# Seven products instead of eight in part of an MLP's first layer, at the end of a fused attention and MLP kernel

## The chip, the cores and the metric

The kernel runs on one core of one Trainium2 chip. A core has engines that work at the same time and wait for one another by semaphores: TensorE (PE in the profile) multiplies matrices into PSUM, a small memory of eight banks, each with room for 128 x 512 f32; VectorE (DVE) and ScalarE (ACT) compute elementwise and read PSUM; GpSimd (POOL) works on SBUF and issues loads; SyncE (SP) issues stores. Each engine takes its instructions strictly in the order in which they were written. The metric is the device time of one execution in microseconds; lower is better. The kernel before takes 332.02 us, the median of six runs from 331.83 to 332.23.

## The reference

```
k_all = concat(beacon_k, k);  v_all = concat(beacon_v, v)       # 16 beacons, then 576 keys
scores = q @ k_all.T / 8, causal for the 576 keys               # 8 batches, 8 heads, 576 x 592, D = 64
x = softmax(scores) @ v_all                                     # to 4608 tokens x 512
h = x @ w_in                                                    # 512 x 2048: the first layer
g = h * sigmoid(1.702 * h)
out = g @ w_out                                                 # 2048 x 512: the second layer, f32
```

## The kernel before, in words

The attention is cut into 16 sets: a batch and four of its eight heads each. A set's scores are computed in chunks of up to 512 columns into one score tile `s` of four banks (`e_qk`, line 458), ScalarE takes the exp of a chunk into the set's buffer `E` in f16 (`e_exp`, line 469; three buffers `E` in all), GpSimd sets the part above the diagonal to zero (line 490), VectorE adds up rows (`e_zadd`, line 508), and TensorE multiplies by ones, for the row sums, and by the values (`e_av`, line 545). VectorE inverts the sums and writes the scaled result to `xT` (`e_norm`, line 580), which is the transposed input of the MLP in f16. There are 55 chunks.

The MLP works on ten groups of tokens: groups 0 and 1 of 256, groups 2 to 9 of 512. In the first layer (`e_m1`, line 604) a group has sixteen n-tiles of 128 columns of `w_in`, each a sum over four k-tiles: four matmuls of 128 x 128 weights by 512 tokens, into one PSUM bank. ScalarE applies the gelu out of the bank into `g` (`e_gelu`, line 625). Group 8 needs tokens of the last batch, group 9 all of it, so both start after nearly all of the attention.

The second layer of groups 2 to 9 already uses Strassen's scheme in Winograd's form: `g` (512 tokens x 2048) and `w_out` (2048 x 512) are cut into two by two quarters, and seven products of quarters stand in for eight. VectorE makes four sums of quarters of `g` in pieces (`e_s`, line 669) and, once, four sums of the weights (`e_t`). A product (`e_prod`, line 718) is sixteen matmuls of 256 columns into one bank. The first product is copied by ScalarE (`e_half`, line 729), and seven VectorE joins (`e_join`, line 734) add the products up to the four quarters of the output, which SyncE stores.

The PSUM banks: four for the score tile, four (`RING`) in a ring that the attention's values, first-layer tiles and second-layer products share.

What runs when is fixed ahead by a planner in the same file (`Plan`). Every operation is entered with its engine, an estimated duration, the operations it depends on, a priority and a due time; `run` then simulates the engines, picks for each the next operation, and the program is emitted in that order. What matters here:

- `quota`: the matmuls of a group's first layer (kind `m1`) are let in once a number of score chunks (`QUOTAS`, for groups 2 to 9) has been issued and the group's input is there; then the planner is `inside`, issues all sixteen n-tiles in a row and no scores. A group is also let in when TensorE would stand idle for more than `IDLE` ns.
- `choose` picks TensorE's next operation: scores first, then values that have been ready for long, then, outside of a group, `m1` and second-layer operations (`m2`, four matmuls each) by turns.
- At most two second-layer banks are open at a time (`allowed`).
- A ring bank becomes free once the operations that close its tile are planned (`ring_free`).
- VectorE takes its operations by priority; it stays idle for up to `NEAR` ns when an urgent one is about to be ready.
- Loads of q, k, v and the transposes have due times that follow a line from `T_ATT0` to `T_ATT1` over the chunks (`due_of`).

Of the kernel before, what the change touches and what calls it, by code (L numbers as in the profile page):

```python
# [12 lines left out]

NEAR = 500
IDLE = 800

# [8 lines left out]
class Plan:  # L25
# [5 lines left out]
    def __init__(self, ring):  # L31
        self.ops = []
        self.bank = [None] * ring
        self.tiles = {}
        self.closers = {}
        self.quota = {}
# [17 lines left out]

    def ring_free(self):
        best = None
        for i, key in enumerate(self.bank):
            t = 0
            for c in self.closers[key] if key is not None else ():
                t = None if t is None or c.start is None else max(t, c.end + 60)  # L60
            if t is not None and (best is None or t < best[0]):
                best = (t, i)
        return best

    def run(self):
# [7 lines left out]
        table, due_of_table = "e", {"e": 0, "g": 0}  # L73
        group, inside, ntile, nchunk = min(self.quota), False, 0, 0
        firsts = {}
        for o in self.ops:
            if o.kind == "m1":
                firsts.setdefault(o.pr, o)

        left_of = {}  # L80
# [4 lines left out]
        def allowed(o):  # L85
            if o.kind == "m2" and o.ring not in self.tiles:
                if sum(left_of[k] > 0 for k in self.tiles if k in left_of) >= 2:
                    return False
            if o.kind == "m1":
                return o.pr < group or (o.pr == group and (inside or group not in self.quota))  # L90
            if o.kind == "qk":
                return not inside
            if o.table is not None and o.table != table:
                return due_of_table[table] == 0
            return True
# [3 lines left out]
        while todo:  # L99
            best = None  # L100
            if not inside and group in self.quota:
                f = firsts[group]
                inside = nchunk >= self.quota[group] and f.left == 0
            slot = self.ring_free()
            ringt = slot[0] if slot else None
            for e, cand in avail.items():
                t = None
                for o in cand:
                    if not allowed(o):
                        continue  # L110
                    r = max(o.ready, o.due)
                    if o.ring is not None and o.ring not in self.tiles:
                        if ringt is None:
                            continue
                        r = max(r, ringt)
                    if t is None or r < t:
                        t = r
                if t is not None:
                    t = max(t, free[e])
                    if best is None or t < best[0]:  # L120
                        best = (t, e)
# [8 lines left out]
            for o in avail[e]:  # L130
                if not allowed(o):
                    continue
                r = max(o.ready, o.due)
                if o.ring is not None and o.ring not in self.tiles:
                    if ringt is None:
                        continue
                    r = max(r, ringt)
                if r <= t:
                    ok.append(o)
            if e == "PE":  # L140
                o = self.choose(ok, t, mode, last, free, inside)
            else:
# [7 lines left out]
            if e == "PE":  # L150
                if o.mode != mode:
                    dur += 95 + 0.75 * tail / 2.4
                mode, last, tail = o.mode, o.kind, o.tail
                if o.ring is not None and o.ring not in self.tiles:
                    self.tiles[o.ring] = slot[1]
                    self.bank[slot[1]] = o.ring
            if o.kind == "m1":
                ntile += 1 if o.pr == group else 0
                if inside and ntile == 16:
                    group, inside, ntile = group + 1, False, 0  # L160
            if o.kind == "m2":
# [29 lines left out]
    def choose(self, ok, t, mode, last, free, inside):  # L191
# [13 lines left out]
        if qk:  # L205
            return qk
        late = first(("av",), lambda o: o.ready + 7000 <= t)
        if late:
# [10 lines left out]
def kernel(  # L219
# [41 lines left out]
    sp = ctx.enter_context(tc.tile_pool(name="sp", bufs=3))  # L261
    pss = ctx.enter_context(tc.tile_pool(name="pss", bufs=1, space=bass.MemoryType.PSUM))
    psu = ctx.enter_context(tc.tile_pool(name="psu", bufs=1, space=bass.MemoryType.PSUM))

    keep = cst.tile([P, P], F16, tag="keep", name="keep")
# [4 lines left out]
    NPL, NPE, GEL = 2, 10, 2  # L270
    QUOTAS = (19, 28, 38, 42, 48, 55, 55, 55)
    HM, HN = 256, NNT // 2
    xT = cst.tile([P, NKT, XR], F16, tag="xT", name="xT")
    sA = [cst.tile([P, HN, HM], F16, tag=f"sA{i}", name=f"sA{i}") for i in range(3)]
# [82 lines left out]

    plan = Plan(RING)

    def ring_tile(key):  # L360
        if key not in rings:
            i = plan.tiles[key]
            rings[key] = psu.tile([P, 512], F32, tag=f"u{i}", name=f"u{i}")
        return rings[key]
# [51 lines left out]
    def f32(ap):  # L416
        return ap.bitcast(F32)
# [173 lines left out]
    NG = len(GROUPS)  # L591

    def e_m1(g, n0, n1):
        t0, t1 = GROUPS[g]
        w = t1 - t0
        if g not in gts:
            gts[g] = gp.tile([P, NNT, 512], F16, tag="g", name="g")
        u = ring_tile(("m1", g, n0))
# [77 lines left out]
    def e_t(i, eng):  # L676
# [9 lines left out]
        else:  # L686
            add(eng, t3, b22, b12, ALU.subtract)

    def quarter(g, i, j):
        return gts[g][:, HN * j : HN * (j + 1), HM * i : HM * (i + 1)]  # L690
# [54 lines left out]

    T_ATT0, T_ATT1 = 17000, 249000
    NCH0 = 4 * HS
# [113 lines left out]
    def values(s):  # L861
# [7 lines left out]
        for i in range(1, NJ if whole else 0):  # L869
            w = S - s0s[i]  # L870
            deps = after(s, wcol[i], wcol[i] + w) + (after(s, Z0, S) if i == 1 else [])
            sums.append(
                op("DVE", 75 + 0.517 * 4 * w, deps + sums[-1:], lambda i=i: e_zadd(s, i), pr=3, name="zadd")
            )
# [72 lines left out]
    m1s, done = {}, {}  # L947
    SQ, SDVE, TDUE = 2, 0, 60000

# [8 lines left out]
    def products(g):  # L958
        eng = "POOL" if g < SDVE else "DVE"
        sd = {}  # L960
        for n0 in range(0, HN, SQ):
            n1 = n0 + SQ
            prev = []
            for i in range(4):
                deps = prev + done.get(g - 1, [])
                for n in range(n0, n1):
                    deps += [gates[(g, n)], gates[(g, n + HN)]]
                d = 336
# [7 lines left out]
        def prod(p):  # L976
            prev = []
            for n0 in range(0, HN, SQ):
# [3 lines left out]
                else:  # L982
                    deps += [gates[(g, n + (HN if p in (2, 4) else 0))] for n in range(n0, n0 + SQ)]
                if rhs[p] is not None:
# [37 lines left out]
        ends[g] = c12  # L1022

    def mlp(g):
        if g == NPL and NPL < NPE:
# [15 lines left out]
        for n0 in firsts:  # L1041
            n1 = n0 + n
            key = ("m1", g, n0)
            pe = op(
# [55 lines left out]
    for o in done.get(NPL - 1, []) + done.get(NPL - 2, []) if tds else ():  # L1100
        also(tds[3], o)
    plan.quota.update(zip(range(GEL, NG), QUOTAS))
    order = plan.run()
# [31 lines left out]
```

## Time and profile before

| | |
|---|---|
| median of the runs | 332.02 us |
| the profiled execution | 331.98 us, its span 330.3 us |
| TensorE busy | 311.5 us, 94% |
| VectorE busy | 237.7 us, 72% |
| ScalarE busy | 203.6 us, 62% |
| GpSimd busy | 116.7 us, 35% |
| first matmul | at 8.6 us |
| first layer of group 8 | 268.1 to 282.0 us |
| first layer of group 9 | 288.2 to 302.0 us |
| last product ends | 326.4 us |

A group of instructions in the profile is named by its line in the code, its engine and operation, then what it writes and reads by the program's names with shapes, then how many there were. TensorE's granted clock is full throughout. Matmuls are pipelined, so one that starts every 109 ns is listed with a longer duration of its own.

### The profile page before, as it was taken

The page shows a single profiled execution, that of the slowest core. Times are in us where ns is not written, and L with a number is a line of the kernel's source. Part 1 is how long each engine was busy: PE and PEld are TensorE (multiplying, and loading weights), DVE is VectorE, ACT ScalarE, POOL GpSimd, SP SyncE. Part 2 cuts the span into 40 slices and gives each one's busy share as a digit, 9 for nine tenths or more (in the row PEclk, how much of TensorE's full clock was granted, in tenths as well). Part 3 has the DMA queues.
Part 4 walks back from the last instruction along what each step waited for, and adds up shares of the span by engine and source line. Part 5 has one row for each costly group of instructions (what it writes and reads, how often), then busy time and mean ns, then how long its engine had stood idle before and what let it go on. Part 6 is the DMA issues. An engine that isn't in the chain of part 4 may idle for free. (4 is left out here: it accounts for less than half of the span.)

```text
span 330.3 us, 9837 instructions
## 1 busy us (share of the span) xinstructions
PE 311.5 (94%) x4288; PEld 211.0 (64%) x4288; DVE 237.7 (72%) x478; ACT 203.6 (62%) x234; POOL 116.7 (35%) x178
## 2 busy tenths in 40 slices
PE   0699899999999999999999999999999999999995
PEld 0477566545885467746878887447774664746884
DVE  3847958796998787987999589978896630460484
ACT  1576487787767786787758586858677426175000
POOL 8764557573238205360427046702422000000000
PEclk9999999999999999999999999999999999999999
DMA  7999999569017903392149623930020000110122
GB/s 127 161 206 208 200 175 151 87 108 131 20 48 134 150 2 82 89 134 44 40 102 126 87 51 89 130 81 2 34 97 2 2 32 2 44 52 2 65 96 95
DMA packets 58219, 28.81 MB, mean 87 GB/s; under 512 B 41280, under 2 KB 53568, under 8 KB 58176
## 3 DMA queue, kind: packets, MB, share of 16 engines
q0 software_dynamic: 47552, 18.49, 47.8%
q1 hardware_dynamic: 10560, 9.69, 8.9%
q8 instruction: 33, 0.54, 0.6%
q14 instruction: 10, 0.08, 0.1%
q10 hardware_dynamic: 64, 0.01, 0.0%
HBM read 37.22 MB, written 9.44 MB: 141 GB/s over the span
## 5 line engine op out<-in xcount | busy, mean ns | idle before, releaser
L604 PE MATMUL u<-xT,w 128*128 128x512 f16 (+1 forms) x704 | 130.8, 343 | 2.1 <-DVE g L637 1.1
L469 ACT ACTIVATE E<-s 128x2048 f16<-128x2048 f32 (+4 forms) x66 | 98.8, 1514 | 42.9 <-PE s L458 42.2
L604 PEld LDWEIGHTS <-w 128*128 128x128 f16 x704 | 67.9, 98 | 58.5 <-issue 3.3
L625 ACT ACTIVATE g<-u 128x512 f16<-128x512 f32 x128 | 74.4, 599 | 43.2 <-PE u L604 43.1
L490 POOL TENSOR_SCALAR_AFFINE_SELECT E<-E 128x512 f16<-128x512 f16 (+3 forms) x78 | 52.0, 688 | 121.9 <-ACT E L469 118.2
L734 DVE SCALAR_TENSOR_TENSOR osb<-u,osb 128x512 f32<-128x512 f32 x56 | 37.4, 680 | 40.5 <-PE u L718 26.9
L718 PEld LDWEIGHTS <-g 128*128 128x128 f16 x512 | 48.7, 98 | 7.3 <-issue 0.2
L458 PE MATMUL s<-qT,kT 32*128 32x32 f16 (+20 forms) x1376 | 36.0, 235 | 12.0 <-DVE qT L429 8.6
L718 PE MATMUL u<-w,g 128*128 128x256 f16 x384 | 46.0, 273 | 0.0
L458 PEld LDWEIGHTS <-kT 32*128 32x128 f16 x1376 | 26.2, 96 | 29.2 <-issue 15.1
L718 PEld LDWEIGHTS <-sA 128*128 128x128 f16 x384 | 36.4, 98 | 4.9
L718 PE MATMUL u<-tB,sA 128*128 128x256 f16 x256 | 31.3, 273 | 0.0
L389 POOL DMA_DIRECT2D vb<-in_v_dram x32 | 27.3, 871 | 2.8 <-DMA kn<-in_k_dram 1.7
L545 PE MATMUL u<-E,vb 128*32 128x352 f16 (+8 forms) x928 | 27.7, 267 | 0.0
L580 DVE TENSOR_TENSOR xT<-u,rz 128x352 f16<-128x352 f32 (+2 forms) x52 | 24.9, 519 | 1.7 <-PE u L545 1.1
L508 DVE TENSOR_TENSOR zs<-zs,E 128x1344 f16<-128x1344 f16 (+2 forms) x36 | 23.2, 645 | 2.7 <-DVE zs L508 0.5
L429 DVE STREAM_TRANSPOSE kT<-kn 128x576 f32<-128x576 f32 x16 | 20.1, 1258 | 4.9 <-PE s L458 2.8
L545 PEld LDWEIGHTS <-vb 128*32 128x32 f16 (+1 forms) x928 | 20.2, 98 | 5.4 <-issue 1.3
L429 DVE STREAM_TRANSPOSE qT<-qn 128x576 f32<-128x576 f32 x16 | 20.0, 1248 | 2.7 <-PE s L458 1.8
L669 DVE TENSOR_TENSOR sA<-g 128x512 f16<-128x512 f16 x32 | 12.8, 417 | 12.3 <-ACT g L625 12.0
L557 DVE STREAM_TRANSPOSE zt<-u 128x352 f32<-128x352 f32 (+2 forms) x32 | 13.8, 459 | 9.0 <-PE u L545 8.9
L718 PE MATMUL u<-tB,g 128*128 128x256 f16 x128 | 16.3, 273 | 0.0
(44 smaller groups left out, 229.6 us busy)
## 6 DMA issues: line engine op xcount, KB each, us to landing
out_dram<-osb SPq DMA_DIRECT2D x36, 256.0 KB, 2.2
kn<-in_k_dram POOLq DMA_DIRECT2D x16, 288.0 KB, 6.0
qn<-in_q_dram POOLq DMA_DIRECT2D x16, 288.0 KB, 6.6
vb<-in_v_dram POOLq DMA_DIRECT2D x24, 128.0 KB, 5.5
w<-in_moe_w_in_dram POOLq DMA_DIRECT2D x8, 256.0 KB, 8.9
w<-in_moe_w_out_dram POOLq DMA_DIRECT2D x4, 512.0 KB, 14.2
vb<-in_v_dram POOLq DMA_DIRECT2D x8, 112.0 KB, 3.6
vb<-in_v_dram POOLq DMA_DIRECT2D x8, 80.0 KB, 5.4
```

The costliest lines, as they stand in the source:

```text
L389: nc.gpsimd.dma_start(out=t[0 : hi - lo, j, h0:h1, :], in_=v[b, h0:h1, lo:hi, :].rearrange("h n d -> n h d"),)
L429: nc.vector.transpose(out=f32(dst.rearrange("p n e -> p (n e)")).rearrange("p (r t) -> p t r", t=TR), in_=f32(src[:, :]).rearrange("p (t c ...
L458: nc.tensor.matmul(sc[:, h, o : o + w], kT[s % NB2][r : r + 32, j * P : (j + 1) * P, d], qT[s % NB2][r : r + 32, a : a + w, d], start=(d = ...
L469: nc.scalar.activation(out=Es[s][:, :, c0:c1], in_=ss[i][:, :, o : o + c1 - c0], func=AFT.Exp, scale=0.125,)
L490: nc.gpsimd.affine_select(out=blk, in_=blk, compare_op=ALU.is_ge, fill=0.0, base=off + (Nb if j == 0 else 0), pattern=[[0, Q], [1, w]], ch ...
L508: nc.vector.tensor_tensor(out=t, in0=E[:, :, Z0:S] if i == 1 else t, in1=E[:, :, wcol[i] : wcol[i] + S - a], op=ALU.add,)
L545: nc.tensor.matmul(u[32 * h : 32 * h + 32, a:e], lhs, src[0:kw, h, col : col + e - a], start=first, stop=last,)
L580: nc.vector.tensor_tensor(out=xT[:, 2 * hs + x : 2 * hs + x + n, t0 : t0 + w], in0=rings[("av", s, x, half)][:, 0 : n * w].rearrange("p (n ...
L604: nc.tensor.matmul(u[:, o + a - t0 : o + e - t0], w1t[:, kp, nt * P : (nt + 1) * P], xT[:, kp, a % XR : (e - 1) % XR + 1], start=(kp == 0) ...
L625: nc.scalar.activation(out=gts[g][:, n0:n1, 0:w], in_=rings[("m1", g, n0)][:, 0 : n * w].rearrange("p (n w) -> p n w", n=n), func=AFT.Gelu ...
L718: nc.tensor.matmul(u[:, HM * mt : HM * (mt + 1)], lhs[:, n, mt * P : (mt + 1) * P], rhs[:, n, :], start=(n == 0 and mt == 0), stop=(n == H ...
L734: nc.vector.scalar_tensor_tensor(out=osbs[(g, dst)][:, :], in0=rings[("p", g, p)][:, :], scalar=scale_of(g), in1=osbs[(g, src)][:, :], op0 ...
```

## The change

Blocks of the first layer of groups 8 and 9 are computed by the same scheme of seven products. A block `d` is the n-tiles 2d, 2d+1, 2d+8 and 2d+9 for the group's 512 tokens. Its quarters are: two k-tiles of `w_in` by two n-tiles, and two k-tiles of `xT` by 256 tokens. `FIRST` lists the blocks: 0 and 2 of group 8, 0, 1 and 2 of group 9; the other three blocks of these groups stay as they were.

- Four sums of halves of `w_in` (128 x 2048, f16) are made once, and four sums of quarters of `xT` (128 x 512, f16) per group, on VectorE. They lie in the `E` buffers of the last sets, once these are no longer read.
- A product (`e_first`) is four matmuls of 256 columns into one bank.
- ScalarE copies the first product to SBUF in f32 (`e_fcopy`). Seven VectorE joins (`e_fjoin`) per block add the others to it, in f32 in the last `E` buffer. Four gelus per block (`e_fgelu`) read the joined quarters from SBUF instead of from a bank.
- The products have four banks of their own, keys that begin with `n`: the score tile's pool is closed and a pool of four one-bank tiles is opened in its place, free for the planner 200 ns after the last exp (`gate`).
- From group 8 on (`MIX`), first-layer operations are allowed whenever they are ready, and `choose` no longer puts them ahead of the second layer.
- Other constants: `NEAR`, `IDLE`, `QUOTAS`, `T_ATT0` and `T_ATT1`, the time after which waiting values go first, `TDUE` (due time of the sums of `w_out`), and the estimate for the row sums.

```diff
-NEAR = 500
-IDLE = 800
+NEAR = 560
+IDLE = 3000
+MIX = 8
+LATE1 = 0
...
-    def ring_free(self):
+    def ring_free(self, late):
         best = None
-        for i, key in enumerate(self.bank):
-            t = 0
+        if late and self.gate.start is None:
+            return None
+        for i in range(self.ring, self.ring + 4) if late else range(self.ring):
+            key = self.bank[i]
+            t = self.gate.end + 200 if late else 0
...
             if o.kind == "m1":
+                if group >= MIX:
+                    return True
                 return o.pr < group or (o.pr == group and (inside or group not in self.quota))
...
-                o = self.choose(ok, t, mode, last, free, inside)
+                o = self.choose(ok, t, mode, last, free, inside and (group < MIX or LATE1))
...
-        late = first(("av",), lambda o: o.ready + 7000 <= t)
+        late = first(("av",), lambda o: o.ready + 5000 <= t)
...
-    QUOTAS = (19, 28, 38, 42, 48, 55, 55, 55)
+    QUOTAS = (20, 27, 33, 33, 47, 54, 55, 55)
     HM, HN = 256, NNT // 2
+    FIRST = {8: (0, 2, ), 9: (0, 1, 2, )}
...
             i = plan.tiles[key]
-            rings[key] = psu.tile([P, 512], F32, tag=f"u{i}", name=f"u{i}")
+            if i >= RING and not late_s:
+                scores.close()
+                late_s.append(ctx.enter_context(tc.tile_pool(name="psl", bufs=1, space=bass.MemoryType.PSUM)))
+            rings[key] = (psu if i < RING else late_s[0]).tile([P, 512], F32, tag=f"u{i}", name=f"u{i}")
...
+    def wq(i, j):
+        return w1t[:, 2 * j : 2 * j + 2, DFF // 2 * i : DFF // 2 * (i + 1)]
+
+    def xq(g, i, j):
+        t0 = (GROUPS[g][0] + HM * j) % XR
+        return xT[:, 2 * i : 2 * i + 2, t0 : t0 + HM]
...
+    def e_first(g, d, p):
+        u = ring_tile(("n", g, d, p))
+        lhs, rhs = {
+            1: (wq(0, 0), xq(g, 0, 0)),
+            2: (wq(0, 1), xq(g, 1, 0)),
+            3: (wsum(2), xq(g, 1, 1)),
+            4: (wq(1, 1), xsum(g, 2)),
+            5: (wsum(0), xsum(g, 0)),
+            6: (wsum(1), xsum(g, 1)),
+            7: (wsum(3), xsum(g, 3)),
+        }[p]
+        for t in range(2):
+            n = (2 * d + t) * P
+            for k in range(2):
+                nc.tensor.matmul(u[:, HM * t : HM * (t + 1)], lhs[:, k, n : n + P], rhs[:, k, :], ...)
+
+    def e_fcopy(g, d):
+        nc.scalar.copy(out=part(d, "m"), in_=rings[("n", g, d, 1)][:, :])
+
+    def e_fjoin(g, d, p, src, dst):
+        nc.vector.tensor_tensor(
+            out=part(d, dst), in0=rings[("n", g, d, p)][:, :], in1=part(d, src), op=ALU.add
+        )
...
-    T_ATT0, T_ATT1 = 17000, 249000
+    T_ATT0, T_ATT1 = -1000, 245000
...
-                op("DVE", 75 + 0.517 * 4 * w, deps + sums[-1:], lambda i=i: e_zadd(s, i), pr=3, name="zadd")
+                op("DVE", 75 + 0.6 * 4 * w, deps + sums[-1:], lambda i=i: e_zadd(s, i), pr=3, name="zadd")
...
-    SQ, SDVE, TDUE = 2, 0, 60000
+    SQ, SDVE, TDUE = 2, 0, 70000
...
+    def first_quarters(g, d, xs, old):
+        every = [(x, h) for x in range(3) for h in range(2)]
+        if not wsums:
+            deps = [avs.get((NSET - 3, x, h)) for x, h in every]
+            for i in range(4):
+                more = [avs.get((NSET - 2, x, h)) for x, h in every] if i == 3 else []
+                wsums.append(op("DVE", 1130, deps + more + wsums[-1:], lambda i=i: e_wsum(i), pr=3, name="wsum"))
+        if (g, 0) not in xsums:
+            deps = xs + [avs.get((NSET - 2, x, h)) for x, h in every]
+            deps += [o for o in m1s.get(g - 2, []) if o.ring[0] == "n"]
+            for i in range(4):
+                xsums[(g, i)] = o = op("DVE", 336, deps, lambda i=i: e_xsum(g, i), pr=2, name="xsum")
...
+        prod(1)
+        m = op("ACT", 480, [last[1], used.get("m")] + free, lambda: e_fcopy(g, d), pr=1, ...)
+        prod(2)
+        c11 = join(2, "m", "a", [m, used.get("a")] + free)
+        ga = gelu("a", 0, 0, c11)
+        prod(6)
+        u2 = join(6, "m", "m", [c11])
+        prod(7)
+        u3 = join(7, "m", "u", [u2, used.get("u")])
+        prod(4)
+        c21 = join(4, "u", "a", [u3, ga])
+        ga = gelu("a", 1, 0, c21)
+        prod(5)
+        u4 = join(5, "m", "m", [u3], False)
+        c22 = join(5, "u", "u", [c21, u4])
+        gu = gelu("u", 1, 1, c22)
+        prod(3)
+        c12 = join(3, "m", "m", [u4])
+        gm = gelu("m", 0, 1, c12)
...
         for n0 in firsts:
             n1 = n0 + n
+            if n0 % HN // SQ in FIRST.get(g, ()):
+                if n0 < HN and n0 % SQ == 0:
+                    first_quarters(g, n0 // SQ, xs, old)
+                continue
...
+    plan.gate = exps[(len(CHUNKS) - 1, len(CHUNKS[-1]) - 1)]
```

## The prediction

> **What bounds the kernel now.** I read the busy shares and the 40 slices first, then the chain that ended last in order of time, TensorE's own waits, and last the instructions in order of time from 260 us on.
>
> ```profile
> PE 311.5 (94%) x4288; PEld 211.0 (64%) x4288; DVE 237.7 (72%) x478; ACT 203.6 (62%) x234; POOL 116.7 (35%) x178
> ...
> PE   0699899999999999999999999999999999999995
> PEld 0477566545885467746878887447774664746884
> DVE  3847958796998787987999589978896630460484
> ```
>
> TensorE is full from about 50 us to 326 us. The stages say where the other 18.8 us are: 8.6 before the first matmul, 4.0 from there to 50 us, 2.3 from 50 us to the last product, and the last 3.9 us, when only a join and a store remain. VectorE is the second engine, but its row ends in low digits: after 260 us it has room. The chain of the last 60 us is TensorE alone:
>
> ```profile
> 266.58 1.54 PE u L545 x56
> 268.13 13.92 PE u L604 x64
> 282.05 6.11 PE u L718 x56
> 288.16 13.81 PE u L604 x64
> 301.97 24.47 PE u L718 x224
> 326.44 0.02 issue
> 326.46 0.69 DVE osb L734
> ```
>
> L604 is the first layer (groups 8 and 9, 64 matmuls each), L718 the Strassen products of the second layer, L545 the attention's last values. No gap stands between them, so a matmul saved here shortens the kernel by its own length as long as the order still finds TensorE something to do. The rows that price the new VectorE work are in order of time:
>
> ```profile
> 282.96 0.69 DVE L734 SCALAR_TENSOR_TENSOR osb<-u,osb 128x512 f32<-128x512 f32 x1 [14.25 <-PE u L718]
> ...
> 286.45 1.29 DVE L734 SCALAR_TENSOR_TENSOR osb<-u,osb 128x512 f32<-128x512 f32 x2 [1.05 <-PE u L718]
> 288.20 0.69 DVE L734 SCALAR_TENSOR_TENSOR osb<-u,osb 128x512 f32<-128x512 f32 x1 [0.46 <-PE u L718]
> 288.81 1.42 DVE L669 TENSOR_TENSOR sA<-g 128x512 f16<-128x512 f16 x4
> ```
>
> A 512-wide f32 join takes 0.69 us alone, and two in a row end after 1.29, so they start about 0.61 apart. Four f16 sums take 1.42, or 0.355 each; alone one is 0.42. VectorE stood idle for 14.25 us while group 8's first layer ran: this is the time that the change spends.
>
> **Matmuls.** Five blocks (d = 0, 2 of group 8 and 0, 1, 2 of group 9) change. Each loses four n-tiles of four 512-wide matmuls: 80 in all, at (13.92 + 13.81)/128 = 216.6 ns, 17.33 us. Each gains seven products of four 256-wide matmuls: 140, at 24.47/224 = 109.2 ns, 15.29 us. Net **-2.04 us**, all on the path. [...] This trace has 216.6 and 109.2 for the same shapes and engine state, so I take the trace. Its weight loads (98 ns each in the groups) just fit beneath 109.
>
> **VectorE, in the tail.** Seven joins a block, 35 in all: 35 x 0.61 = 21.4 us packed, 35 x 0.69 = 24.2 us if each pays its full length. [...] Eight sums of x: 8 x 0.355 = 2.8 to 8 x 0.42 = 3.4 us. Now the room. Group 9's last five products need all sums of group 9, and take 5 x 16 x 0.109 = 8.7 us; so the window runs from the first matmul of group 8 (268.1) to 326.4 - 8.7 = 317.7, less the 2.04 saved: 47.6 us. VectorE's old work in it is 0.66 + 2.67 + 6.05 + 4.06 (its busy time in 268-282, 282-288, 288-302, 302-314) plus one join and sixteen sums after 314 (0.7 + 5.7), 19.8 us. With the new 24.2 to 27.6 it is **44.0 to 47.4 of 47.6 us**. It fits with 0.2 to 3.6 us to spare, but VectorE must scarcely ever stand still, and joins in one block read what the one before wrote (7 after 6, 4 after 7), which costs more than 0.61. What queues behind a late join is the late bank (four for 35 products), then the product that wants it, and in TensorE's strict order everything after it. Cost to TensorE between 0 and 3.5 us; I take **+0.8**, nearer the packed rows, because from group 8 on first-layer and second-layer operations alternate (the branch for `inside` is off) and the plain blocks bring no joins. If that mixing fails and 21 products of group 9 come together at 0.44 us each, joins at 0.61 would hold TensorE by 21 x 0.17 = 3.6 us.
>
> **Sums of the weights.** Four of 2048 f16 elements: the second layer's like sums took 1.21 to 1.30 us, so 4.9 us. They need the values of set 13 (the last one also 14) to be over. VectorE has 3.4 idle in 250-260 and 3.6 in 260-268, so I cost them at nothing; without that cover each may put off the attention's row sums by 1.2 us, and the group-8 matmuls behind them.
>
> **ScalarE.** Five copies at 0.60 = 3.0 us, and as many gelus as before, now read from SBUF. It is busy 18.5 of the 34 us from 268 to 302: nothing. What is late if a copy is late is the first join of its block, already counted. No new table load: all gelus of groups 8 and 9 come after the last exp. **Banks**: the score tile is last read when the exp at 244.6 ends at 246.5, over 20 us before the late banks are wanted: nothing. No DMA is added.
>
> **The new order.** Other constants re-plan everything. Due times change from 17.0 + 4.936 per chunk to -1.0 + 5.234 us, so loads and transposes may go 16 us sooner at chunk 16 and 6 us sooner at chunk 48. They pass other POOL issues (0.57 us for q and k, 0.87 for v) and VectorE work of lower urgency, and could feed TensorE in its 4.0 us of early holes, or crowd DMA engines that are 90% busy there. First-layer groups start sooner (quota 38 to 33, 42 to 33, 55 to 54), a hole of up to 3 us no longer lets one in early (`IDLE`), values that wait go first after 5 us instead of 7, VectorE may stand still 0.56 us for urgent work instead of 0.50, and the row sums are planned longer. The sums of the second layer's weights are held until 70 us instead of 60: they ended at 68 and are first read at 86.2, so ten more hide. The work of TensorE stays; its changes of tiling mode, some 144 by the order of its matmuls, cost about 0.1 us each (1.85 us in the chain where sixteen products need 1.75), so ten more or fewer are 1 us. Bounds -2 to +2; with nothing that favours a side I take **0**.
>
> **Sum.** The profiled run took 331.98 us, a span of 330.3 and 1.7 around it, next to the shown median of 332.02. 331.98 - 2.04 + 0.8 = **330.7 us**.
>
> **Rivals.** I call a difference under 0.2% (0.66 us) no change.
> A, the likeliest (0.47): as summed; TensorE keeps most of the saving, 329.4 to 331.3.
> B (0.13): joins eat the saving. VectorE loses 2 to 4 us of its window to waits, TensorE stalls about 2 us, 331.4 to 332.6. For it: 44 to 47.4 of 47.6. Against: group 7's products may be moved later, each giving 1.75 us of TensorE for one join.
> C, slower (0.19): VectorE becomes the bound of the last stage. It decides once TensorE's stalls pass 2.04 + 0.66 = 2.7 us, that is, once VectorE stands idle or runs over by 2.9 us (joins at 0.69) or 6.3 us (at 0.61) in the window. With 21 joins bunched it is 3.6 us: 331.98 - 2.04 + 3.6 = 333.5; up to 335. Against it: VectorE's current idleness is spread over the whole window.
> C2, slower too (0.13): a hole at the attention's end. Group 7's first layer, with quota 54, may come before the last score chunk. Before, that layer (13.9 us) and 56 products (6.1) covered the way from the last scores (244.5) to the last norm. Its shortest form is exp, masks and row sums 6.1 (until 250.6), ones 0.8, reciprocals 2.1, values with their norms 2.2: 11.2 us. Group 7's 112 products alone give TensorE 12.2 us, but VectorE would owe sixteen sums (5.7), row sums (3.9), reciprocals (2.1), norms (1.7) and seven joins (4.3) in them: 17.7. No hole if the sums are done before, up to 17.7 - 12.2 = 5.5 us if not; with half of that, 330.7 + 2.7 = 333.4. It decides beyond 1.9 us. Against it: group 6's leftovers can cover too.
> D (0.08): the new order also fills early holes and the joins cost nothing: 327.5 to 329.3.
> So faster 0.47 + 0.08 = 0.55, same 0.13, slower 0.32. Range 329.0 to 334.4: about 0.05 of D lies below, about 0.12 of the slower cases above.
>
> **What would show it.** First-layer matmuls: 512-wide ones fall from 448 to 368, and a new line has 140 of 256 at about 109 ns; otherwise the first step is wrong. TensorE's waits on the new joins should total under 1.5 us; VectorE's busy time should rise by 30 us (21.4 to 24.2 + 3 + 4.9) to about 268, mostly after 245 us. C would show as long waits of TensorE for joins; C2 as TensorE waiting for norms or sums just before the first Strassen product; D as fewer idle us in 10-50. What would make me wrong above all is a tail where VectorE is busy 9 tenths while TensorE is not.

## The result, and the profile after

| | before | after |
|---|---|---|
| median | 331.86 us (40 runs, 331.58 to 333.96) | 334.11 us (19 runs, 332.93 to 334.71) |
| ratio | | 1.0056, interval 1.0046 to 1.0066 |
| the profiled execution | 331.98 us, span 330.3 | 334.68 us, span 332.9 |
| TensorE idle from 50 to 325 us | 2.3 us | 4.8 us |
| first Strassen product of the first layer | | at 278.3 us |
| last product ends | 326.4 us | 329.1 us |

The change made the kernel 0.56% slower, where a gain of 0.4% was forecast; the time lies in the forecast range. Ratios, here and below, go by the means (here 333.86 and 332.00 us). The 20 executions of the changed kernel whose clock is on record fall in two lots: 12 show a mean granted clock of 0.993 to 0.995 and take 333.7 to 334.7 us (median 334.4), 8 show 0.997 to 1.000 and take 332.7 to 333.4 (median 333.0). Both medians are above that of before.

Busy shares and slices of the kernel after, from the page:

```profile
PE 311.5 (94%) x4348; PEld 217.4 (65%) x4348; DVE 264.9 (80%) x525; ACT 209.3 (63%) x241; POOL 115.3 (35%) x178
...
PE   0699899979999999999999999899999999999995
PEld 0477566534786468645878877447864686678784
DVE  3747968679899868969696959986997669899983
```

TensorE's busy time is 311.5 us as before, although 2.0 us of matmul time were taken out of it; the slow layer shown below puts 1.6 us back. VectorE went from 237.7 to 264.9 us, and the low digits at the end of its row are gone. So far this looks like the rival in which VectorE becomes the bound of the last stage. TensorE's own waits say otherwise (us in total, times, longest):

```profile
PE s L476 <- DVE qT L447: 10.8, 2, 8.5
PE s L476 <- ACT E L487: 3.5, 5, 2.0
...
PE u L773 <- DVE E L785: 0.3, 1, 0.3
```

L773 is the new line of products, L785 the new joins (35 of them with a mean of 683 ns, together 22.7 us of busy time). For all joins together TensorE waited **0.3 us**. The windows of the last stage show the two side by side (PE, weight loads, DVE, ACT, POOL, then clock, DMA share and GB/s):

```profile
290.00:300.00 10.00, 9.73 (x80) 7.59 (x79) 9.80 (x21) 5.68 (x10) 0.00 (x0) 1.00 0.07 24
300.00:310.00 10.00, 10.00 (x94) 8.96 (x93) 9.76 (x17) 5.27 (x9) 0.00 (x0) 1.00 0.10 33
```

VectorE is busy 98% of these 20 us, and TensorE 99%: a bound just not reached. The tail even gained: before, from the first matmul of group 8 (268.06) to the end took 58.4 us, of which 6.1 were products of group 7, 52.3 net; after, from the first product (278.28) to the end (329.10) it is 50.8, or **-1.5 us**. So the loss lies ahead of it: the last two groups begin 4.1 us later than they did (278.28 against 268.06 + 6.11).

The largest piece stands at 66 us, far from the change. TensorE in order of time, after:

```profile
65.96 0.66 PE L476 MATMUL s<-qT,kT 32*128 32x336 f16 x24 [0.15 <-ACT E L487]
68.62 0.72 PE L476 MATMUL s<-qT,kT 32*128 32x384 f16 x24 [2.01 <-ACT E L487]
69.28 15.53 PE L626 MATMUL u<-xT,w 128*128 128x512 f16 x64
```

and before:

```profile
65.90 0.66 PE L458 MATMUL s<-qT,kT 32*128 32x336 f16 x24 [0.38 <-ACT E L469]
66.50 3.63 PE L604 MATMUL u<-xT,w 128*128 128x512 f16 x16
70.48 10.52 PE L604 MATMUL u<-xT,w 128*128 128x512 f16 x48 [0.35 <-ACT g L625]
```

Before, group 2's first layer (64 matmuls) follows the nineteenth score chunk at once. After, a twentieth chunk is put ahead of it; there is one score tile, so that chunk waits 2.01 us until the exp of the one before (66.69 to 68.57 us, 1.88 us long) has read it. And what follows is slow: the same 64 matmuls take 15.5 us instead of 13.9. The windows give the reason:

```profile
66.00:68.60 2.60, 0.61 (x24) 0.45 (x24) 0.00 (x0) 2.32 (x2) 2.60 (x5) 1.00 1.96 137
68.60:72.00 3.40, 3.38 (x31) 1.50 (x31) 3.24 (x4) 2.60 (x3) 3.40 (x6) 0.56 1.45 204
```

For 3.4 us behind the hole the granted clock is 0.56. The hole and the clock together are 3.6 us. The kernel before had waits of its own at this place (0.38 and 0.35 us, against 0.15 left), so about 3.0 us of the 4.1 are new here. Most of the remainder is spread over small waits of 0.2 to 0.5 us: from 100 to 278 us TensorE is idle for 2.4 us, against 1.5 before.

### The profile page after: what moved, and what is told of

The parts are those of the page before. It is cut to its first block, busy times and chain, and to the rows that moved or that the text cites. A ratio compares the mean times of both kernels' runs of the same rounds, so it can differ in the third digit from the quotient of the medians.

```text
span 332.9 us, 10023 instructions
## 1 busy us (share of the span) xinstructions
PE 311.5 (94%) x4348; PEld 217.4 (65%) x4348; DVE 264.9 (80%) x525; ACT 209.3 (63%) x241; POOL 115.3 (35%) x178
## 4 chain that ended last, share of the span: by engine, by line
PE 76%; DVE 9%; ACT 6%; DMA 4%; issue 3%; POOL 1%; SPq 1%; DVEq 0%; POOLq 0%
PE u L626 29%; PE u L826 25%; PE s L476 8%; PE u L563 7%; ACT E L487 4%; PE u L773 4%; PE u L671 3%; DMA qn<-in_q_dram 2%; DMA bkf<-in_beacon_k_dram 2%; DVE E L785 1%; DVE osb L842 1%; DVE qT L447 1%; DVE rz L586 1%; DVE zs L526 1%; DVE zt L575 1%
## 5 line engine op out<-in xcount | busy, mean ns | idle before, releaser
L626 PE MATMUL u<-xT,w 128*128 128x512 f16 (+1 forms) x624 | 117.0, 341 | 1.7 <-DVE g L659 0.9
L508 POOL TENSOR_SCALAR_AFFINE_SELECT E<-E 128x512 f16<-128x512 f16 (+3 forms) x78 | 50.6, 671 | 138.5 <-ACT E L487 136.6
L626 PEld LDWEIGHTS <-w 128*128 128x128 f16 x624 | 60.8, 99 | 46.7 <-issue 4.5
L647 ACT ACTIVATE g<-u 128x512 f16<-128x512 f32 x108 | 63.4, 597 | 31.0 <-PE u L626 30.6
L826 PE MATMUL u<-w,g 128*128 128x256 f16 x384 | 48.5, 273 | 0.0
L842 DVE SCALAR_TENSOR_TENSOR osb<-u,osb 128x512 f32<-128x512 f32 x56 | 37.4, 678 | 12.7 <-PE u L826 6.7
L826 PE MATMUL u<-tB,sA 128*128 128x256 f16 x256 | 32.8, 273 | 0.0
L526 DVE TENSOR_TENSOR zs<-zs,E 128x1344 f16<-128x1344 f16 (+2 forms) x36 | 24.3, 675 | 2.7 <-POOL E L508 0.5
L575 DVE STREAM_TRANSPOSE zt<-u 128x352 f32<-128x352 f32 (+2 forms) x32 | 13.9, 464 | 15.7 <-PE u L563 15.6
L785 DVE TENSOR_TENSOR E<-u,E 128x512 f32<-128x512 f32 x35 | 22.7, 683 | 1.7 <-PE u L773 1.2
L526 DVE TENSOR_TENSOR zs<-E 128x1856 f16<-128x1856 f16 x12 | 15.6, 1300 | 6.8 <-ACT E L487 5.3
```

Of the source, the lines that this page charges most:

```text
L508: nc.gpsimd.affine_select(out=blk, in_=blk, compare_op=ALU.is_ge, fill=0.0, base=off + (Nb if j == 0 else 0), pattern=[[0, Q], [1, w]], ch ...
L526: nc.vector.tensor_tensor(out=t, in0=E[:, :, Z0:S] if i == 1 else t, in1=E[:, :, wcol[i] : wcol[i] + S - a], op=ALU.add,)
L626: nc.tensor.matmul(u[:, o + a - t0 : o + e - t0], w1t[:, kp, nt * P : (nt + 1) * P], xT[:, kp, a % XR : (e - 1) % XR + 1], start=(kp == 0) ...
L647: nc.scalar.activation(out=gts[g][:, n0:n1, 0:w], in_=rings[("m1", g, n0)][:, 0 : n * w].rearrange("p (n w) -> p n w", n=n), func=AFT.Gelu ...
L785: nc.vector.tensor_tensor(out=part(d, dst), in0=rings[("n", g, d, p)][:, :], in1=part(d, src), op=ALU.add)
L826: nc.tensor.matmul(u[:, HM * mt : HM * (mt + 1)], lhs[:, n, mt * P : (mt + 1) * P], rhs[:, n, :], start=(n == 0 and mt == 0), stop=(n == H ...
```

## The experiments

Each diff below is an edit of the changed kernel, unless said otherwise. All compare with before at 331.65 to 331.84 us on the same chip.

**The blocks in the old order.** All of the planner's constants as before, the Strassen blocks as in the change; the sums of the first layer's weights get the lowest urgency.

```diff
-NEAR = 560
-IDLE = 3000
+NEAR = 500
+IDLE = 800
...
-        late = first(("av",), lambda o: o.ready + 5000 <= t)
+        late = first(("av",), lambda o: o.ready + 7000 <= t)
...
-    QUOTAS = (20, 27, 33, 33, 47, 54, 55, 55)
+    QUOTAS = (19, 28, 38, 42, 48, 55, 55, 55)
...
-    T_ATT0, T_ATT1 = -1000, 245000
+    T_ATT0, T_ATT1 = 17000, 249000
...
-    op("DVE", 75 + 0.6 * 4 * w, ..., name="zadd")
+    op("DVE", 75 + 0.517 * 4 * w, ..., name="zadd")
...
-    SQ, SDVE, TDUE = 2, 0, 70000
+    SQ, SDVE, TDUE = 2, 0, 60000
...
-    wsums.append(op("DVE", 1130, ..., pr=3, name="wsum"))
+    wsums.append(op("DVE", 1130, ..., pr=6, name="wsum"))
```

> The five blocks as in the changed kernel, but with all planner constants of the kernel before, and the four weight sums at VectorE's lowest priority. Theory (the tail gained, and the re-planned order lost it earlier, in a 2.0 us gap of TensorE at 66.7 us and in the low clock after it): no such gap, first layers of groups 2 to 6 where they were before, 332.0 less the 1.5 us that the tail of the changed kernel shows or the 2.0 of the matmuls, so 330.0 to 330.5 us. Rival (the joins cost the tail more than the matmuls save): 332 to 334 us, with TensorE waiting for joins.

Measured: **329.66 us** (329.61 to 329.86), ratio 0.9936 (0.9923 to 0.9948). It beats both kernels. Its last product ends at 324.1 us, 2.3 earlier than before; 0.3 of it is a first matmul at 8.3 instead of 8.6, so the blocks give -2.0. Its window from 290 to 300 us:

```profile
290.00:300.00 10.00, 10.00 (x94) 8.95 (x93) 9.69 (x19) 4.86 (x9) 0.00 (x0) 1.00 0.08 26
```

TensorE is full, with VectorE at 97%. From 262 to 324 us TensorE waits for nothing. The blocks are worth what the matmul term says, and the joins cost nothing.

**The new order alone.** The kernel before, with only the new constants; no block.

> The kernel before, all first-layer blocks plain, with only the constants of the changed kernel; the program is the changed kernel's up to about 240 us. Theory: the gap at 66 to 69 us and the low clock after it are there without any of the new products, so 3.6 us above the kernel before, about 335.5 us, or a few more if the end of the attention leaves a hole too. Rival (the order does no harm, the products do): 331.5 to 332.5 us.

Measured: **335.87 us** (335.28 to 336.49), ratio 1.0122 (1.0106 to 1.0137): +4.0 from the constants by themselves. The same hole and the same slow layer:

```profile
68.16 0.96 PE L458 MATMUL s<-qT,kT 32*128 32x384 f16 x24 [2.00 <-ACT E L469]
69.06 15.28 PE L604 MATMUL u<-xT,w 128*128 128x512 f16 x64
```

With it the two parts are separate: -2.2 for the blocks, +4.0 for the order, +1.8 in sum. Measured for both is +1.9 by the means; the medians give +2.3, since the median of the changed kernel lies in the lot with the low clock.

**The hole filled.** Nine matmuls of 512 columns, which nobody reads, go into a bank of the ring ahead of the twentieth chunk; then, in a second kernel, five.

```diff
+        if i == 19:
+            fill = psu.tile([P, 512], F32, tag="u3", name="u3")
+            for _ in range(9):
+                nc.tensor.matmul(fill[:, :], w1t[:, 0, 0:P], xT[:, 0, 0:512], start=True, stop=True)
```

> The changed kernel with nine 512-wide matmuls, whose result nobody reads, put into the 2.0 us gap before the twentieth score chunk, into a ring bank that is free there. If idleness of TensorE lowers the clock: the granted clock stays full in 68 to 72 us, group 2's 64 matmuls take 13.9 us and not 15.5, and the time falls by about 1.5 us to 332.6, with the gap itself still lost. If the low clock has another cause: 334.1 as before the filling. If the matmuls delay the score chunk: 334.1 or more with a full clock.

> The changed kernel with five instead of nine unread matmuls in the 2.0 us gap before the twentieth score chunk; some 0.9 us stay idle, and the matmuls come first. If the clock answers to a gap of about 2 us only: granted clock full after it as with nine, 333.3 us. If 0.9 us is enough: a low clock in 68 to 72 us in most executions, about 334.1.

Measured: 333.26 us with nine (333.04 to 333.29, ratio 1.0041, 1.0028 to 1.0055), 333.23 with five (333.00 to 333.42, 1.0044, 1.0029 to 1.0059). The gain by the medians, 0.85 us, is short of the 1.5 that I expected of nine: the low clock comes in only 12 of 20 executions of the changed kernel, and the 8 without it take 333.0 us with no filling at all. Profiled execution against profiled execution (334.68, 333.20) the gain is 1.5. TensorE with five, and the window behind:

```profile
65.96 1.25 PE L470 MATMUL u<-xT,w 128*128 128x512 f16 x5
68.03 0.64 PE L480 MATMUL s<-qT,kT 32*128 32x384 f16 x24 [0.82 <-ACT E L491]
```

```profile
68.60:72.00 3.40, 3.40 (x28) 1.58 (x17) 3.31 (x4) 3.23 (x4) 3.10 (x5) 1.00 1.33 186
```

A hole of 0.8 us here leaves the clock full, and so does none at all (with nine the clock is 1.00 in the same window). Neither fill lets the chunk start before the exp has ended (68.24 us with nine, 68.03 with five). The low clock is thus shown as a part of the loss: 0.85 us of the median, where the wait for the exp, by the trace, is 2.0 us.

**One constant at a time.** Is one constant to blame? First IDLE alone in the kernel before (800 to 3000, so the planner may stand still for 3 us before it begins a group's first layer):

> The kernel before with one constant changed, the planner's limit for a gap on TensorE raised from 800 to 3000 ns. Theory: where the first layer of a group used to be let in at a gap, the planner now lets TensorE stand still for an exp; one gap of about 2 us comes before group 3 near 103 us, with a low clock in the 3 us after it in some executions, and a shorter one near 140 us: 334 to 337 us. If this constant is harmless: 331.8.

Measured: **340.72 us** (339.92 to 340.86), ratio 1.0265 (1.0250 to 1.0280), more than I had expected. Its holes are elsewhere:

```profile
105.23 0.65 PE L458 MATMUL s<-qT,kT 32*128 32x400 f16 x24 [1.98 <-ACT E L469]
106.88 0.38 PE L545 MATMUL u<-zs,ones 128*32 128x352 f16 x8 [1.00 <-DVE zs L508]
```

and the clock is 0.63 from 108 to 112 us. This pointed at IDLE, so I put it back alone in the changed kernel, and in another the first quota alone (20 chunks to 19). Either removes the hole at 66 us without any unread matmul.

```diff
-IDLE = 3000
+IDLE = 800
```

```diff
-    QUOTAS = (20, 27, 33, 33, 47, 54, 55, 55)
+    QUOTAS = (19, 27, 33, 33, 47, 54, 55, 55)
```

> The changed kernel with IDLE alone put back from 3000 to 800; quotas, due times and the blocks stay as changed. Theory 'one stand-still of 2 us and its clock': group 2's first layer starts in the hole at 66 us as before, so 2.0 us of gap and 0.9 to 1.4 us of low clock go, 334.1 to 330.7 to 331.2. Rival 'the patient constant is all of it': the small later waits go too, about 329.7 as with all old constants. Rival 'the other new constants cost as much': 333 or more, with holes elsewhere.

> The changed kernel with only the first quota put back from 20 score chunks to 19, so that group 2's first layer may start before the twentieth chunk; IDLE stays 3000. Theory 'one stand-still of 2 us and its clock': the gap at 66.6 us goes without any unread matmul, 330.7 to 331.2. Rival 'a planner that may stand still 3 us makes such gaps wherever it is let': new gaps elsewhere (more than 1.5 us of TensorE idle in some stage after 75 us), 333 to 336.

Measured: **337.36 us** (336.57 to 338.39; ratio 1.0171, 1.0150 to 1.0191) and **336.12 us** (335.27 to 337.13; 1.0131, 1.0109 to 1.0153). In both runs the theory of one stand-still falls: the hole at 66 us is gone, and the kernel is 2 to 3 us slower than with it. The rivals with holes elsewhere hold. TensorE in order of time with the quota back:

```profile
94.49 0.66 PE L476 MATMUL s<-qT,kT 32*128 32x256 f16 x32
...
99.19 0.38 PE L563 MATMUL u<-zs,ones 128*32 128x352 f16 x8 [1.17 <-DVE zs L526]
...
105.41 0.64 PE L476 MATMUL s<-qT,kT 32*128 32x448 f16 x16 [2.08 <-ACT E L487]
```

The chunk at 94.49 came at 91.22 before. It had to wait for the transposes of its queries, and VectorE in order of time shows where they stood:

```profile
79.73 1.22 DVE L691 TENSOR_TENSOR tB<-w,tB 128x2048 f16<-128x2048 f16 x1
...
93.18 1.25 DVE L447 STREAM_TRANSPOSE qT<-qn 128x576 f32<-128x576 f32 x1
```

The first of these is the last of the four sums of the second layer's weights (1.2 us each, from 73.0 us on here; before the change the last of them began at 67.8). Joins, norms and row sums stand between the two. While the chunk is late, the products that should have covered later chunks are, as I read it, used up, and from 97 to 106 us TensorE stands still 4.1 us. Hence the next runs: those sums released at 60 us again, in the changed kernel and in the one with the quota back.

```diff
-    SQ, SDVE, TDUE = 2, 0, 70000
+    SQ, SDVE, TDUE = 2, 0, 60000
```

> The changed kernel with the sums of the second layer's weights released at 60 us again instead of 70. Theory 'late sums crowd VectorE': the four sums of 1.2 us no longer stand in the stage of 68 to 100 us, where VectorE was busy 23 of 25 us; but in the changed order the stand-still at 66.6 us stays, so the gain is small: 332.8 to 334.0. Rival 'the release time matters little': 334.1 as before it.

> The changed kernel with the first quota back at 19 and the release of the weight sums back at 60 us. With the quota alone the time was 336.1, with 4.1 us of TensorE idle between 97 and 106 us, where a score chunk had come 3.3 us late because the transpose of its queries ran at 93.2 us, behind the weight sums and joins on VectorE. Theory 'late sums crowd VectorE': the chunk comes on time, at most 1 us idle there, 331 to 333. Rival 'the sums are innocent': 335.5 to 336.5.

Measured: 334.48 us (333.41 to 334.77; 1.0068, 1.0054 to 1.0082) in the changed kernel, no gain; and 334.10 us (333.74 to 335.68; 1.0080, 1.0062 to 1.0098) with the quota back, 2.0 less than with the quota alone (1.6 by the means: two of the six executions take 335.5 to 335.7, at a mean clock of 0.995). The transpose of the queries now runs at 85.28 us instead of 93.18. So the late sums do make the holes at 97 to 106 us, of which 0.4 are left, but the time stays above the forecast for that theory: a new hole of 1.5 us stands at 139 us, where the first layer of a group waits for the normed values.

Last, the old due times alone, and four constants back together (first quota, IDLE, the release at 60 us, the due times), which leaves new only the other quotas, the look-ahead of 0.56 us, values first after 5 us, the planned length of the row sums and the urgency of the first layer's weight sums.

```diff
-    T_ATT0, T_ATT1 = -1000, 245000
+    T_ATT0, T_ATT1 = 17000, 249000
```

> The changed kernel with the old due times alone (17.0 + 4.936 us a chunk instead of -1.0 + 5.234). Theory 'early loads and transposes pass other VectorE and GpSimd work': 331 to 333. Rival 'due times cost nothing': 333.7 to 334.5. If the constants only work together: slower than 334.7.

> The changed kernel with four of its new constants back: first quota 19, IDLE 800, the weight sums' release at 60 us, the old due times. What is left new are the other quotas, the look-ahead of 0.56 us, values first after 5 us, and the planned length of the row sums. If the four are the loss: 329.5 to 330.5, as with all constants back (329.66). If the rest has a part: 331 to 334.

Measured: 334.51 us (334.26 to 335.56; 1.0085, 1.0073 to 1.0098), so the due times alone are no gain either, and 333.88 us (333.61 to 334.12; 1.0059, 1.0047 to 1.0071). Even with four back nearly the whole loss remains ("the rest has a part"), in other places:

```profile
209.91 11.81 PE L626 MATMUL u<-xT,w 128*128 128x512 f16 x54 [1.03 <-DVE xT L598]
...
278.08 0.60 PE L773 MATMUL u<-E 128*128 128x256 f16 x4 [0.65 <-DVE E L691]
279.28 0.60 PE L773 MATMUL u<-E 128*128 128x256 f16 x4 [0.60 <-DVE E L691]
```

The waits at 278 us are for the sums of x: group 7's products are used up by 274 us, and the chain norm, sum, product is bare.

The orders side by side, by the profiled execution: TensorE's idle time between 50 and 325 us (without the 0.9 us after the last product in the first row), and the time lost to a low clock, (1 - granted clock) times the width of the windows of 9 or 50 us that show it, so only to a few tenths.

| order | time, us | idle, us | low clock, us | holes of 0.9 us or more |
|---|---|---|---|---|
| blocks, all constants old | 329.64 | 2.3 | 0 | none |
| all new (the changed kernel) | 334.68 | 4.8 | 1.7 | 66 |
| release back | 334.51 | 5.2 | 1.7 | 66 |
| quota and release back | 333.74 | 5.4 | 0 | 139 |
| four back | 333.91 | 5.3 | 0 | 209 |
| due times back | 334.26 | 6.4 | 0 | 66 |
| quota back | 336.12 | 7.0 | 1.5 | 98, 103 to 105 |
| IDLE back | 338.39 | 8.5 | 1.5 | 99, 104 to 106, 277 |
| no blocks, all old (before) | 331.98 | 2.3 | 0 | none |
| no blocks, all new | 336.31 | 5.2 | 1.7 | 66 |

In the seven rows with blocks and other constants, idle time and low clock account, against the first row, for 3.0 of 4.3 us ("four back") to 4.6 of 4.9 us ("release back"). What remains, 0.3 to 1.3 us, is the start (first matmul at 8.3 to 9.0 us) and changes between kinds of matmuls; I did not take it apart.

**More blocks.** In the old order, six blocks (d = 1 of group 8 too), then all eight.

```diff
-    FIRST = {8: (0, 2, ), 9: (0, 1, 2, )}
+    FIRST = {8: (0, 1, 2), 9: (0, 1, 2)}
```

```diff
-    FIRST = {8: (0, 2, ), 9: (0, 1, 2, )}
+    FIRST = {8: (0, 1, 2, 3), 9: (0, 1, 2, 3)}
```

> As the first kernel of this set (constants of the kernel before, weight sums last), with six blocks: 0, 1, 2 of group 8 and 0, 1, 2 of group 9. If VectorE still has room in the tail: another 0.41 us less than with five, some 329.6 to 330.1. If VectorE is at its limit with five: the seven further joins (4.3 to 4.8 us) come back as waits of TensorE, 330.5 to 334.

> As the kernel with the old constants and five blocks (329.7 us), but all eight blocks of groups 8 and 9 by seven products. If joins were free: 3 x 0.41 less, 328.4 us. Theory (VectorE is within a few us of its limit in the tail: 90% busy with five blocks, 97% with six): 21 more joins at 0.61 to 0.69 are 12.8 to 14.5 us for 3 x 3.46 us of plain blocks that brought it none, so TensorE waits for joins and late banks and the time is above 332, some 334 to 338 us: the slower rival of the forecast, at more blocks than the change has.

Measured: **329.82 us** with six (329.31 to 330.24; 0.9939, 0.9927 to 0.9952), no gain over five that this spread would show (the first matmul of the profiled execution comes at 8.72 us, with five at 8.26); **335.99 us** with eight (335.88 to 336.11; 1.0126, 1.0109 to 1.0143). With eight, one window, and TensorE's wait for joins:

```profile
280.00:290.00 10.00, 8.89 (x72) 6.47 (x70) 10.00 (x21) 4.44 (x8) 0.00 (x0) 1.00 0.09 31
```

```profile
PE u L773 <- DVE E L785: 1.5, 6, 0.3
```

Here VectorE has no idle time, and TensorE waits 1.5 us for joins in all, 1.1 for sums of g (L691) and 0.7 for a copy. From 280 us to the last product TensorE is idle for 3.9 us; with five blocks it was idle for none. That is the rival "VectorE becomes the bound", shown, with three blocks more than the change has. It is a part of the 6.3 us between eight blocks and five; the rest I did not take apart. With five, a VectorE busy for 97% (old order, 290 to 300 us) cost nothing, and one busy for 98% (the changed kernel, 290 to 310 us) the 0.3 us of waits.

**No mixing.** In the old order, group 8 and 9's first-layer matmuls ahead of the second-layer products instead of in turn with them.

```diff
-LATE1 = 0
+LATE1 = 1
```

> The kernel with the old constants and five blocks, but inside of groups 8 and 9 first-layer operations go ahead of the second layer again: products come in bunches, and eleven second-layer operations of group 7 after group 8. If mixing is what hides the joins: TensorE waits for joins and late banks, 1 to 3.6 us above 329.7, so 330.7 to 333.3. If the plain tiles and the four late banks suffice: 329.5 to 329.9.

Measured: **330.32 us** (330.05 to 330.71; 0.9957, 0.9943 to 0.9972), +0.66 over the mixed order, between the two things expected. In the profiled execution 0.34 of it is a first matmul at 8.60 instead of 8.26 us, ahead of anything that the edit touches; the last product ends 0.67 later (324.77, 324.10). So the mixing is worth 0.3 to 0.7 us, and TensorE's waits for joins, 0.2 us in this run, can be most of it or little.

## Why the prediction was wrong, by its steps

**Matmuls, -2.04: right.** -2.0 measured on the last product in the old order. The trace's 216.6 and 109.2 ns were the right ones: in the tail of the changed kernel four 512-wide matmuls take 0.87 us (313.25 to 314.12), 217 ns each, and 28 matmuls of 256 columns, by fours of new products and of the second layer in turn, 3.05 us (294.80 to 297.85), 109 ns each.

**VectorE in the tail, +0.8: too dear.** It is 0 in the old order, and 0.3 us of waits in the changed one. The size of the new work was right (joins 22.7 us, forecast 21.4 to 24.2; VectorE 264.9 us in all, forecast about 268). The room was not: in the old order VectorE was busy for 42.3 of the 46.7 us from 268.7 to 315.4, where 44.0 to 47.4 of 47.6 were forecast, so it could stand still for 4.4 us and did. The old work was put too high, 19.8 us; the trace of before shows 16.9 us busy from 268.1 to 317.7, and its last four sums run until 320.9, behind the end that I had set for them. My sign for being wrong, a tail with VectorE busy nine tenths while TensorE is not, did not come: where VectorE was at 98% (290 to 310 us), TensorE was at 99. The 3.6 us for the case that mixing fails were too dear: without mixing the kernel lost at most 0.7.

**Sums of the weights, ScalarE, banks, at nothing: right** in the old order, with the sums at the lowest urgency. No run with five blocks shows TensorE waiting for the weight sums.

**The new order, 0 with bounds of -2 to +2: this is the step that failed.** It measured **+4.0** without the blocks and +4.45 with them (334.11 - 329.66; +4.1 by the means), twice the bound. Three things in it were wrong. "a hole of up to 3 us no longer lets one in early" was read and not priced; a 2.0 us hole is what it allowed, and 1.7 us of low clock behind it were not thought of. "so ten more hide" was said of the later release of the weight sums from when they are first read (86.2 us), and not of what they push back on VectorE: with the quota back, a transpose of queries, with it a score chunk, and up to 2.0 us of time. (They ended at 69.0 us, not 68.) And the balance, "nothing that favours a side", was the real mistake. The trace of before had 2.3 us of idle TensorE from 50 us on and 4.0 between the first matmul and 50 us: the idle time left is a limit on what filling holes can win, and there is no such limit on what can be lost. Of the early 4.0 us the new order won 0.2 (TensorE busy 37.6 us from 8 to 50 us without the blocks, 37.4 before). So the profile gave no ground for bounds that are alike on both sides.

**The rivals.** C (VectorE the bound) and C2 (a hole at the attention's end) end on the right side, but neither is what happened: joins 0.3 us, and 0.41 us just before the first product. The loss sits in the attention's stages, where no rival looked. That 334.11 lies in the forecast range is luck: the upper part of the range stood for these two, and a loss from joins or at the attention's end is not what filled it. C2's place has 1.5 us of idle time in "four back" and 2.8 in "IDLE back" (268 to 285 us): a hole of its size, in orders that are not the change's.

**What stays open.** No single constant is the cause. Going back on one or four of them removed the hole it explains and left the kernel at 333.9 to 337.4 us; only all of them gave 329.66. Which pair or group decides, I did not find; nor did I separate, in the old order, the urgency of the weight sums from the rest.

## What to carry to other kernels

When an edit brings a new order with it, run the edit in the old order and the new order without the edit: two runs here split the +1.9 us (by the means) into -2.2 and +4.0. A planner's constants fit together, and one of them taken back is a third order, not a measurement of that constant. Before giving a new order zero, read how much idle time the bounding engine has left: that limits what filling holes can gain, and nothing limits the loss.

## What I had not expected of the hardware

A hole of 2.0 us in TensorE's work can be followed by half its clock: 0.50 in both windows of 1 us from 70 to 72 us of the changed kernel, full again from 73 us on. By the mean clock it came in 12 of 20 executions. In the profile of "IDLE back" the mean clock from 100 to 150 us is 0.97, and the 54 matmuls behind a hole of only 1.45 us (and three of 0.4 to 1.2 us in the 6 us ahead of it) take 13.72 us, where 54 in "four back" take 11.81:

```profile
105.90 13.72 PE L626 MATMUL u<-xT,w 128*128 128x512 f16 x54 [1.45 <-DVE xT L598]
```

The length of one hole does not decide it. The profile of "due times back" has the same hole of 2.00 us at 68.2 and a full clock (1.00 from 66 to 75 us), and so has the kernel before, near its start, with 1.00 in every us from 12 to 21:

```profile
11.67 1.04 PE L458 MATMUL s<-qT,kT 32*128 32x288 f16 x24 [2.04 <-ACT E L469]
```

A hole of 0.8 us at 67 us left the clock full (1.00 from 66 to 72 us, with five unread matmuls). In the changed kernel the low clock lasted about four us (0.52, 0.50, 0.50 and 0.78 in the four us from 69 to 73), and after its first matmul TensorE was never idle for longer than 2.4 us on end. Why it came in 12 executions of 20 and not in the other 8, no run shows.

VectorE can be busy 96 to 97% for 20 us beside a full TensorE at no cost (290 to 310 us in the old order). At 99 to 100% it may cost or not: with eight blocks TensorE was idle for 11.1% of 280 to 290 us, with VectorE busy 100%, and for nothing from 300 to 310 us, with VectorE busy 98.7%.
